# Moving every large operand buffer to the same address remainder as the weights

## The chip, the cores and the metric

The kernel runs on one core of a Trainium2 chip. The metric is the device time of one execution in microseconds (us). A core has a matrix engine (TensorE, PE in the profile, with its weight loads shown apart as PEld), a vector engine (VectorE, DVE), a scalar engine (ScalarE, ACT), GpSimd (POOL) and a queue engine that issues the transfers (SyncE, SP). On-chip memory (SBUF) has 128 partitions; a buffer takes the same range of bytes in each of them, and the addresses below are bytes within a partition.

## The reference

Four sequences of 576 tokens, eight heads of 64. The attention is masked by blocks of 64 tokens; its output, 2304 tokens of 512 features, goes through two feed-forward layers.

```
scores = where(block_i >= block_j, q k^T / 8, -1e9)      # per batch and head, 576 x 576
x = softmax(scores) v                                    # -> 2304 x 512
x = (sigmoid(x Wg) * (x Wv)) Wout                        # 512 -> 1536 -> 512
out = leaky_relu(x Win, 0.01) Wout2                      # 512 -> 2048 -> 512
```

## The kernel before

Every operand of a feed-forward product is kept as two parts, a high one and a low one, and a product of two tiles is three matmuls: high weights by high data, high weights by low data, low weights by high data (the loop over `wl, xl`, lines 1294 and 1142). The weights are the stationary operand (128 by 128), the data the moving one (up to 512 columns).

The 2304 tokens are three slices of 768, 512 and 1024 columns. The profile shows them as three stages. In stage 1 (about 50 to 364 us) and stage 2 (364 to 640 us) `half_unit` (line 1276) runs units of 12 matmuls, at 512 columns or, for the first 256 columns of the slice of 768, at 256. Units of kind gate, val and h read the layer's input; units of kind y and o read the intermediate `g`. Pieces of the attention of the later tokens stand between them. In stage 3 (from about 640 us) `pair_unit` (line 1109) multiplies the last 1024 columns as 2 by 2 blocks with seven products (`B11`, `T1`, `T2`, `B21`, `T3`, `B22`, `T4`) in place of eight; each product is two triples of matmuls at 512 columns. Its sums of blocks lie in buffers that stages 1 and 2 used before.

`Plan.order` (line 157) writes out one order of all instructions from fixed costs and due times, before the program is built. It knows no addresses.

Where a buffer lies: the program lays its pools out one behind the other in the order in which they are made, the constant tiles first, and rounds each start up to a multiple of 32 bytes. In the program before, the starts, and what is left of them after multiples of 256, are:

| remainder | buffers that TensorE reads |
|---|---|
| 32 | `w` (all weights, 63776 and on), `g`, `qk`, `v`, and in stage 3 `raw` (37152 and on) |
| 0 | `x1` (20736): input of stage 2; blocks `T1` and `B21` of stage 3 |
| 96 | `x0` (145760) and `xa` (162144): input of stage 1, `xa` also block `B22`; `sg` (170336): part of the intermediate of kind o, some blocks; `both` (182624): the attention's probabilities, blocks `B11`, `T2`, `T3`, `T4`; `acc` (215392): some blocks of stage 3 |
| 128 | `last` (16512) and `ident` (19072): two small operands of the attention |

All slices that the matmuls take from these buffers begin at a multiple of 256 bytes from the buffer's start. In the trace the names lose their numbers: `x` is `x0` and `x1`; below 364 us it is `x0`, later `x1`.

The names `mm`, `sc`, `tp` and `pa` are the banks that a matmul writes to, not what it computes: in stage 3 the feed-forward products of line 1147 write to `sc`, `tp` and `mm`.

Of the kernel before, what the change touches and what calls it, by code (L numbers as in the profile page):

```python
# [8 lines left out]
F32 = mybir.dt.float32  # L9
# [9 lines left out]
P = 128  # L19
# [205 lines left out]
def block_attention_then_two_mlps(  # L225
# [30 lines left out]
    def pool(name, bufs, **k):  # L256
        return ctx.enter_context(tc.tile_pool(name=name, bufs=bufs, **k))

    def ring(name, bufs, shape, dtype=F32, **k):
        return Ring(pool("p_" + name, bufs, **k), bufs, shape, dtype, name)  # L260

    out_hbm = out
    const = pool("const", 1)
# [19 lines left out]

    ident = const.tile([P, P], F32, name="ident")
    mask = const.tile([P, 4 * P + BLK], BF16, name="mask")
    x1 = const.tile([P, 4, 2, TN], F32R, name="x1")
    r_x = ring("x0", 4, [P, 2 * TN])
    r_xa = ring("xa", 2, [P, 4 * CUT])
    x0, xa, xt = [r_x.tile(F32R) for _ in range(4)], [r_xa.tile(F32R) for _ in range(2)], []
# [1159 lines left out]
    with tc.manual_schedule():  # L1449
        make_identity(nc, ident)  # L1450
        nc.gpsimd.memset(p_l[BLK:, (NKT - 1) * P:], 0.0)
        nc.gpsimd.memset(mask, 0.0)
        nc.gpsimd.memset(mask[:BLK, 4 * P:], MASK)
        warm = const.tile([P, 1], F32, name="warm")
        nc.vector.memset(warm, 0.0)
        nc.scalar.activation(warm, warm, AF.Exp)
        for o, e in plan.order():
            for t in o.uses:
                if t.ap is None:
                    t.ap = t.ring.pool.tile(t.ring.shape, t.dtype, name=t.ring.name)  # L1460
            if o.either:
                o.fn(e)
            else:
                o.fn()
# [39 lines left out]
```

## Time and profile before

| | us |
|---|---|
| median of 3 runs | 995.12 (994.21 to 996.48) |
| the profiled execution, as timed | 994.91 |
| its span in the trace | 993.1 |
| TensorE busy | 977.9 (98%) |
| VectorE busy | 779.5 (78%) |
| ScalarE busy | 550.3 (55%) |

The time as timed is 1.8 us above the span: what lies before the first and behind the last instruction. TensorE is busy in nearly the whole span and its granted clock is at full speed in all 40 slices of the page. A matmul's shown duration holds the time that it waits in the pipe behind its predecessor, so how fast matmuls follow each other is read from the difference of two starts, divided by the number of matmuls between them. The timeline below merges neighbours of one line and one name into one row, with the count behind.

### The profile page before, as it was taken

How to read it: one execution, taken by the hardware profiler on the slowest of the kernel's cores; microseconds unless marked ns; L12 is line 12 of the kernel's file. 1: busy time of each engine (PE TensorE's matmuls, PEld its weight loads, DVE VectorE, ACT ScalarE, POOL GpSimd, SP SyncE). 2: the span in 40 equal slices, each digit the busy share in tenths (PEclk: the TensorE clock that was granted, in tenths of full speed). 3: DMA queues.
4: the chain of work that ended last, by engine and by line, in shares of the span. 5: the costliest groups of instructions: out<-in, count | busy, mean ns of one | idle time of the engine just before them, and what ended most of it. 6: DMA issues, size and time to landing. Idle time of an engine off the chain costs nothing.

```text
span 993.1 us, 15675 instructions
## 1 busy us (share of the span) xinstructions
PE 977.9 (98%) x5468; PEld 779.7 (79%) x5468; DVE 779.5 (78%) x1658; ACT 550.3 (55%) x1103; POOL 166.1 (17%) x172
## 2 busy tenths in 40 slices
PE   7999999999999999999999999999999999999998
PEld 4688888878888878778777777788888877888886
DVE  6989989889989847777689888966437489958656
ACT  7988776676766526464566565443525144643521
POOL 2422001221102001232332223021002021100000
PEclk9999999999999999999999999999999999999999
DMA  8499786756876537979997877876565555665554
GB/s 207 135 292 270 264 289 219 258 186 242 265 258 197 208 116 268 299 273 298 281 296 266 303 265 243 280 267 220 173 200 186 187 170 160 204 204 182 193 185 154
DMA packets 92718, 227.52 MB, mean 229 GB/s; under 512 B 9952, under 2 KB 29920, under 8 KB 92640
## 3 DMA queue, kind: packets, MB, share of 16 engines
q1 hardware_dynamic: 92640, 226.53, 69.5%
q8 instruction: 43, 0.70, 0.3%
q14 instruction: 35, 0.29, 0.1%
HBM read 150.47 MB, written 76.02 MB: 228 GB/s over the span
## 4 chain that ended last, share of the span: by engine, by line
PE 94%; DVE 3%; DMA 1%; ACT 1%; SPq 0%; issue 0%; POOL 0%; DVEq 0%; ACTq 0%
PE mm L1299 48%; PE sc L1147 17%; PE tp L1147 9%; PE mm L1147 4%; PE tp L631 3%; PE sc L426 3%; PE pa L655 2%; PE tp L426 2%; PE tp L567 1%; DMA qk<-in_qk 1%; PE mm L655 1%; PE tp L582 1%; DMA w<-ds 1%; DVE x L1219 0%; SPq L330 0%; DVE g L353 0%
## 5 line engine op out<-in xcount | busy, mean ns | idle before, releaser
L1299 PE MATMUL mm<-x,w 128*128 128x512 f32 (+2 forms) x1008 | 236.9, 387 | 0.0
L1299 PEld LDWEIGHTS mm<-x,w 128*128 128x128 f32 x1008 | 179.8, 188 | 40.8 <-issue 5.2
L1299 PE MATMUL mm<-g,w 128*128 128x512 f32 (+1 forms) x792 | 164.0, 358 | 0.0
L1299 PEld LDWEIGHTS mm<-g,w 128*128 128x128 f32 x792 | 130.0, 189 | 23.4 <-issue 2.3
L1147 PE MATMUL sc<-both,w 128*128 128x512 f32 x480 | 130.6, 396 | 0.1
L1147 PEld LDWEIGHTS sc<-both,w 128*128 128x128 f32 x480 | 90.1, 188 | 21.8 <-ACT wf L340 0.5
L498 ACT ACTIVATE both<-both,nm 128x256 f32<-128x256 f32 (+5 forms) x148 | 84.1, 570 | 29.7 <-DVE nm L483 29.1
L899 POOL TENSOR_TENSOR wf<-mag,rnd 128x512 int32<-128x512 int32 x28 | 37.4, 1335 | 204.3 <-DVE w L353 149.5
L885 ACT ACTIVATE mag<-raw 128x512 f32<-128x512 f32 x68 | 45.5, 670 | 43.9 <-DVE wf L899 18.0
L1299 PE MATMUL mm<-xa,w 128*128 128x256 f32 x480 | 62.7, 281 | 0.0
L1299 PEld LDWEIGHTS mm<-xa,w 128*128 128x128 f32 x480 | 59.9, 188 | 3.3 <-issue 0.8
L353 DVE TENSOR_TENSOR g<-gf,g 128x512 fp32r<-128x512 f32 (+2 forms) x73 | 57.8, 793 | 3.5 <-ACT g L340 3.4
L518 POOL TENSOR_SCALAR both<-both,r 128x256 f32<-128x256 f32 (+6 forms) x54 | 34.9, 652 | 116.4 <-DVE r L511 97.0
L340 ACT ACTIVATE g<-gf 128x512 fp32r<-128x512 f32 (+2 forms) x61 | 40.0, 657 | 23.6 <-DVE gf L1330 11.9
L516 ACT ACTIVATE both<-both,r 128x384 f32<-128x384 f32 (+6 forms) x94 | 48.6, 566 | 6.9 <-DVE r L511 6.9
L483 DVE CUSTOM_DVE_ANT_0 both<-sc,mask 128x256 f32<-128x256 f32 (+6 forms) x101 | 39.4, 423 | 15.9 <-PE sc L426 15.8
L1360 DVE TENSOR_TENSOR acc<-mm,acc 128x512 f32<-128x512 f32 (+1 forms) x60 | 35.7, 598 | 18.1 <-PE mm L1299 17.7
L1219 DVE TENSOR_TENSOR x<-sc,x 128x512 f32<-128x512 f32 x44 | 30.2, 689 | 23.2 <-PE sc L1147 23.2
L426 PE MATMUL sc<-qk 64*128 64x384 f32 (+5 forms) x228 | 42.2, 415 | 5.9 <-DMA qk<-in_qk 5.9
L893 DVE SCALAR_TENSOR_TENSOR mag<-raw,mag 128x512 int32<-128x512 int32 x68 | 47.4, 698 | 0.3
L1299 PE MATMUL mm<-sg,w 128*128 128x512 f32 (+1 forms) x216 | 47.4, 355 | 0.0
L353 DVE TENSOR_TENSOR w<-wf,w 128x512 fp32r<-128x512 f32 x68 | 46.5, 684 | 0.2
(255 smaller groups left out, 1851.0 us busy)
## 6 DMA issues: line engine op xcount, KB each, us to landing
w<-wd SPq DMA_DIRECT2D x102, 512.0 KB, 4.6
raw<-in_w SPq DMA_DIRECT2D x68, 512.0 KB, 4.5
wd<-w SPq DMA_DIRECT2D x68, 512.0 KB, 4.2
ds<-raw SPq DMA_DIRECT2D x68, 512.0 KB, 5.2
w<-ds SPq DMA_DIRECT2D x68, 512.0 KB, 4.3
qk<-in_qk SPq DMA_DIRECT2D x32, 288.0 KB, 6.3
w<-wd SPq DMA_DIRECT2D x68, 128.0 KB, 3.8
v<-in_v SPq DMA_DIRECT2D x32, 160.0 KB, 3.5
```

The costliest lines, as they stand in the source:

```text
L340: nc.scalar.activation(dst(), src(), AF.Copy)
L353: engines[e].tensor_tensor(dst(), a(), f32(b()), ALU.subtract)
L426: nc.tensor.matmul(ps[row:row + nq, col:col + nk], lhsT=tqk[half, 0, q0:q0 + nq], rhs=tqk[half, 1, k0:k0 + nk], start=True, stop=True,)
L483: nc.vector.tensor_tensor_reduce(out=pt[:, n:n + width], in0=ps[:, col:col + width], in1=mask[:, 4 * P + BLK - width:] if masked else mask ...
L498: nc.scalar.activation(pt[:, :n], pt[:, :n], AF.Exp, bias=nm[:, k - 1:k], scale=-1.0, accum_out=sm[:, i:i + 1],)
L516: nc.scalar.activation(pt[:, :n], pt[:, :n], AF.Copy, scale=r[:, i:i + 1])
L885: op("act", c_act(n), lambda: nc.scalar.activation(mag[:], words(1).bitcast(F32), AF.Abs), [raw], [mag], [raw, mag], d - 8)
L893: op("dve", c_dve(n), lambda: nc.vector.scalar_tensor_tensor(out=mag[:].bitcast(I32), in0=words(1).bitcast(I32), scalar=-0x40000000, in1=m ...
L899: engines[e].tensor_tensor(wf[:].bitcast(I32), mag[:].bitcast(I32), rnd[:], ALU.add)
L1147: nc.tensor.matmul(p[:, :n], lhsT=wt[:, wl, at * P:(at + 1) * P], rhs=view[:, xl], start=first and k == 0 and wl + xl == 0, stop=k == 1 an ...
L1299: nc.tensor.matmul(ps[:, :n], lhsT=ws[:, wl, k * P:(k + 1) * P], rhs=srcs[k]()[:, xl, hs], start=k == 0 and wl + xl == 0, stop=k == 3 and ...
L1360: op("dve", c_dve(n), lambda: nc.vector.tensor_tensor(a(), ps[:, :n], a(), ALU.add), [ps], toks_a, [ps, *host], e)
```

## The change

A tile of 4 bytes, `warm`, is made before `x1` and no longer behind all other constants, and a pool with one tile of 48 floats (192 bytes), which nothing writes or reads, is made between `x1` and `x0`. Instructions, their order and their operands stay as they are; only addresses differ.

```
@@ constants and rings
     ident = const.tile([P, P], F32, name="ident")
     mask = const.tile([P, 4 * P + BLK], BF16, name="mask")
+    warm = const.tile([P, 1], F32, name="warm")
     x1 = const.tile([P, 4, 2, TN], F32R, name="x1")
+    pool("even", 1).tile([P, 48], F32, name="even")
     r_x = ring("x0", 4, [P, 2 * TN])
...
@@ before the planned order is issued
         nc.gpsimd.memset(mask[:BLK, 4 * P:], MASK)
-        warm = const.tile([P, 1], F32, name="warm")
         nc.vector.memset(warm, 0.0)
         nc.scalar.activation(warm, warm, AF.Exp)
```

## Rows read from the trace of the kernel before

**Rows 1.** The page, busy time: engine, us, share of the span, instructions.

```profile
PE   977.9 (98%) x5468; PEld 779.7 (79%) x5468; DVE 779.5 (78%) x1658; ACT 550.3 (55%) x1103; POOL 166.1 (17%) x172
```

**Rows 2.** The page, the chain that ended last, by engine.

```profile
PE 94%; DVE 3%; DMA 1%; ACT 1%; SPq 0%; issue 0%; POOL 0%; DVEq 0%; ACTq 0%
```

**Rows 3.** Timeline of TensorE in stage 3: start, us, line, operands, count.

```profile
645.98 11.07 PE L1299 MATMUL mm<-g,w 128*128 128x512 f32 x48
656.88 0.86 PE L1147 MATMUL tp<-x,w 128*128 128x512 f32 x3
...
700.29 0.86 PE L1147 MATMUL tp<-xa,w 128*128 128x512 f32 x3
...
712.18 0.40 PE L1147 MATMUL sc<-g,w 128*128 128x512 f32 x1
...
737.13 0.85 PE L1147 MATMUL sc<-both,w 128*128 128x512 f32 x3
...
741.93 0.62 PE L1147 MATMUL tp<-x,w 128*128 128x512 f32 x2
...
764.31 2.96 PE L1147 MATMUL sc<-both,w 128*128 128x512 f32 x12
...
769.91 0.40 PE L1147 MATMUL sc<-g,w 128*128 128x512 f32 x1
...
975.85 0.86 PE L1147 MATMUL mm<-raw,w 128*128 128x512 f32 x3
...
978.62 0.84 PE L1147 MATMUL mm<-raw,w 128*128 128x512 f32 x3
...
985.42 1.52 PE L1147 MATMUL sc<-g,w 128*128 128x512 f32 x6
```

**Rows 4.** Timeline of TensorE in stage 2, attention pieces between the units.

```profile
455.80 3.04 PE L1299 MATMUL mm<-x,w 128*128 128x512 f32 x12
458.67 0.93 PE L631 MATMUL tp<-ident,both 128*128 128x128 f32 x7
...
462.59 8.65 PE L1299 MATMUL mm<-x,w 128*128 128x512 f32 x36
471.17 0.70 PE L426 MATMUL sc<-qk 64*128 64x256 f32 x4
...
487.03 3.00 PE L1299 MATMUL mm<-g,w 128*128 128x512 f32 x12
489.87 0.93 PE L631 MATMUL tp<-ident,both 128*128 128x128 f32 x7
...
493.76 5.74 PE L1299 MATMUL mm<-g,w 128*128 128x512 f32 x24
499.34 0.86 PE L1299 MATMUL mm<-x,w 128*128 128x512 f32 x3
```

**Rows 5.** Timeline of TensorE in stage 1; a merged row can hold both widths.

```profile
103.57 1.58 PE L1299 MATMUL mm<-xa,w 128*128 128x256 f32 x12
...
107.73 1.58 PE L1299 MATMUL mm<-xa,w 128*128 128x256 f32 x12
...
124.37 16.88 PE L1299 MATMUL mm<-g,w 128*128 128x256 f32 x96
...
141.18 0.92 PE L426 MATMUL sc<-qk 64*128 64x384 f32 x4
```

**Rows 6.** Groups of TensorE by line and shape: count, busy us, mean ns.

```profile
L1299 PE MATMUL mm<-x,w 128*128 128x512 f32 x912 | 223.5, 397 | 0.0
...
L631 PE MATMUL tp<-ident,both 128*128 128x128 f32 x304 | 42.8, 274 | 0.8 <-ACT both L340 0.8
L1299 PE MATMUL mm<-sg,w 128*128 128x512 f32 x144 | 37.2, 393 | 0.0
```

**Rows 7.** Stretches: busy us (count) of each engine, granted clock, transfers.

```profile
656.90:990.00 333.10, 329.99 (x1417) 265.22 (x1415) 222.42 (x347) 135.69 (x225) 29.38 (x22) 1.00 0.59 192
...
820.00:840.00 20.00, 19.05 (x77) 13.65 (x76) 19.62 (x32) 8.72 (x15) 4.21 (x3) 1.00 0.56 179
```

More of the change, by code (lines that the diff above doesn't have):

```diff
@@ L285, in block_attention_then_two_mlps @@
     mask = const.tile([P, 4 * P + BLK], BF16, name="mask")
+    warm = const.tile([P, 1], F32, name="warm")
     x1 = const.tile([P, 4, 2, TN], F32R, name="x1")
+    pool("even", 1).tile([P, 48], F32, name="even")
     r_x = ring("x0", 4, [P, 2 * TN])
@@ L1453, in block_attention_then_two_mlps @@
         nc.gpsimd.memset(mask[:BLK, 4 * P:], MASK)
-        warm = const.tile([P, 1], F32, name="warm")
         nc.vector.memset(warm, 0.0)
```

## The prediction

> **What bounds the kernel now.** I read the page's busy times first: TensorE is busy 98% of the span, VectorE 78% [rows 1]. The chain that ended last says the same of the path: 94% of it is TensorE's own work [rows 2]. So the time is, to a few per cent, the sum of what its 5468 instructions take one behind the other, and a change that touches no instruction can only act through how closely matmuls follow each other. That is read from the timeline, as the difference of two starts over the count between them, and compared by the remainder of the moving buffer's address.
>
> Stage 3 gives all classes at 512 columns with the same weights [rows 3]:
> - Remainder 32, the weights' own: 48 matmuls on `g` from 645.98 to 656.88 take 10.90 us, 227.1 ns each. From 975.85 to 978.62 a run that mixes `raw`, `qk` and `g` needs 2.77 us for 12, 230.8 ns each; then, from 978.62 to 985.42, 6.80 us for 30, 226.7 ns. So such a run starts slow, for some nine to twelve matmuls, and settles.
> - Remainders 0 and 96 in turn, the usual case of this stage: 700.29 to 712.18, 51 matmuls in 11.89 us, 233.1 ns.
> - Remainder 96 alone: 21 in 4.80 us from 737.13 (228.6 ns), but 24 in 5.60 us from 764.31 (233.3 ns). It has two paces and does not leave the slow one in 24 matmuls.
>
> Remainder 0 alone stands in stage 2: 36 matmuls on `x1` from 462.59 to 471.17, 8.58 us, of which about 0.17 is the slow restart at both ends (how I get it is below): 233 to 234 ns [rows 4]. The buffers with the good remainder are of four kinds and the pace is one, so I take the address, not what the tile holds, for the cause.
>
> **What the change does to addresses.** `warm` (4 bytes, rounded to 32) now lies before `x1`: 20736 + 32 = 20768, which is 81 x 256 + 32. The constants keep their total, so `raw` to `v` with the weights stay at 32. The filler's 192 bytes bring `x0` from 145760 to 145952 = 570 x 256 + 32, and `xa`, `sg`, `both` and `acc` behind it go from 96 to 32 as well. The end moves from 227680 to 227872. `ident` and `last` stay at 128, so "every buffer" holds for the large ones only. No instruction is added, removed or moved; no wait, transfer or queue place changes.
>
> **Stage 3.** Between 656.9 and 990 TensorE is busy 329.99 us with 1417 instructions, 232.9 ns each [rows 7]. At 226.7 all 1428 products of this stage would save 1428 x 6.2 = 8.8 us. From that goes:
> - 1.9 us for the 21 places of this stage (counted in the timeline) where a product waited or restarted and its first matmul is followed late, at 0.09 us each, the restart of stage 2 (below); that excess is in the mean and stays;
> - 0.5 us for settling again at about a dozen separate ones, 9 matmuls by 4 to 5 ns each, from the run at 975.85;
> - 0.6 us in the one part where VectorE is the bound: from 820 to 840 it is busy 19.62 of 20.00 us and TensorE only 19.05 [rows 7], and the stretch before looks alike. What some 30 us of products gain there, 2%, comes back as waiting.
>
> Left: 5.8 us. The bounds are 8.8 - 1.9 = 6.9 (settled at once, nothing given back) and 4.4 (VectorE gives back 2% of 100 us and not of 30).
>
> **Stage 2.** Here units of 12 are cut apart by transposes of the attention. Behind such a cut, 12 on `x1` take 455.80 to 458.67, 2.87 us, and 12 on `g` take 487.03 to 489.87, 2.84 us [rows 4]: the unit ends about when the good pace is reached, and 0.03 is all. 2.87 against 12 x 233 = 2.80 gives the restart of 0.07 to 0.09. Later units of one run gain more: the second of the 24 on `g` from 493.76 to 499.34 takes 5.58 - 2.84 = 2.74, where a later one of the 36 on `x1` takes (8.58 - 2.87 - 0.09) / 2 = 2.81: 0.07. Of the 912 matmuls on `x` at 512 columns [rows 6] 480 are on `x1` (the 40 units gate, val and h by 12). About 29 units begin a run and 11 do not (counted in the timeline): 29 x 0.03 + 11 x 0.07 = 1.6 us. The bounds: 0.9 (0.03 each, rounded down, for all) and 3.1 (480 x 6.4 ns, settled at once).
>
> **Stage 1.** The units alternate 12 matmuls at 256 columns and 12 at 512. On `xa` and `x0`, remainder 96, one takes 107.73 - 103.57 = 4.16 us. On `g`, remainder 32, four take 141.18 - 124.37 = 16.81, less 0.09 for the cut behind the last, 4.18 each [rows 5]. So the change costs 0.02 on each of 40 units: 0.8 us lost; between 0 and 1.6 from what the starts, printed to 0.01, allow over 40 units. What the 512 columns gain once they settle, the 256 columns give away.
>
> **The rest.** 144 matmuls on `sg` at 512 columns [rows 6] go from 96 to 32: 0.3 us gained, between 0 (they stay unsettled) and 0.9 (6.6 ns each). Transposes with `both` as the weights (304 of them in the largest group [rows 6], 408 in all) and the products of probabilities and `v`, some 380 instructions, also see `both` move. No row shows them at another remainder; the nearest are the classes of the wide products, whose ends are 6.4 ns apart over 512 columns and which in stage 1 cancel. I take 0, and plus or minus 2 us (3 ns by the sum of both, some 790) as ends. VectorE's and ScalarE's operands in these buffers move too; TensorE covers them nearly everywhere, I take 0.
>
> **Sum.** 5.8 + 1.6 + 0.3 - 0.8 = 6.9 us. Against the profiled execution's own 994.91 us (span 993.1 and 1.8 around it) that is 988.0; the median of the runs shown is 0.2 us above that execution, so I say 988.2.
>
> **Rivals.**
> 1. *Nothing changes, 995.1.* For it: the paces may belong to the mixture of buffers, the order of reads or the settled state before, not to the address; 96 alone shows both 228.6 and 233.3 [rows 3], so the remainder isn't the whole story. Against it: no run at 32 longer than a dozen stays slow, and no run on `x1` gets fast. 8%. The page "SBUF — State Buffer" of the Trainium skill, in "Who interferes with whom", says that TensorE's two read ports are its own and independent and that "PE and ACT never wait on anyone"; by that rule no address could slow a matmul and this rival would hold. The three paces in this trace, 226.7, 228.6 and 233 ns for one shape, speak against it.
> 2. *The gain is given back as waiting, 991.2.* If VectorE holds TensorE not in 30 but in 100 us of stage 3, and stage 2 gains nothing because its units are released by transfers and VectorE, what is left is 4.4 + 0.3 - 0.8 = 3.9 us: 995.1 - 3.9 = 991.2. For it: VectorE is at 19.62 of 20 us in one place and at 222 of 333 over the stage [rows 7], so other places can be like it. Against it: the chain has only 3% VectorE and 1% transfers [rows 2]. 12%.
> 3. *Slower, 999.* One mechanism: the settled pace is lost when blocks of different hosts follow each other, because equal remainders make weights and data meet more often than before. Then all 32s run at their first dozen's pace: in stage 3 the matmuls that now run at 226.7 or 228.6 go to 231 to 233, some 2 us lost; stage 1 loses the 1.6 of its bound and stage 2 about 0.4 on its `g` units: 995.1 + 4 = 999. It decides from the point where no run gets past its first twelve. For it: the first 12 from 975.85 at 230.8 ns. Against it: that very run goes on over three kinds of buffer and settles. 5%.
>
> **How the numbers follow.** The forecast has 75%, the rivals 8, 12 and 5. Its own range, from the bounds of the terms, is 985 to 991: stage 3 up to 1.1 more, stage 2 1.5 more, `sg` 0.6 on the good side not all at once, 2 us either way for the attention, against 1.4 and 0.7 less in stages 3 and 2 on the bad side. Rival 2 lies at its edge, so 985.0 to 991.6 holds eight cases in ten. A difference under 0.2% (2.0 us, the spread of the runs shown is 2.3) can't be told from none. Faster by more than that: the forecast and nearly all of rival 2, 0.86; the same: 0.09; slower: 0.05.
>
> **What would show it.** In stage 3, runs over changing buffers at 226.7 ns, so that triples stand 0.68 us apart and not 0.70, and the run that now begins at 975.85 begins about 6 us earlier; TensorE's busy sum from 656.9 on down by 6 us; stage 2 shorter by 1.6 to 2; units of stage 1 at 4.18 and not 4.16. The prediction is wrong if triples on `both` or `x1` still stand 0.70 apart, if rows with a wait on VectorE grow by more than 2 us in stage 3, or if transposes have another distance than now.

## The result and the profile after

The changed kernel takes 987.93 us (median of 4 runs, 986.15 to 988.29) against 995.65 before (4 runs, 994.21 to 996.48): a ratio of 0.992 with a 95% interval of 0.9903 to 0.9938. The forecast was 988.2. The profiled execution took 986.15 us, its span is 984.4.

First the page, busy time and the chain; they answer to [rows 1, 2].

```profile
PE 969.9 (99%) x5468; PEld 780.4 (79%) x5468; DVE 778.8 (79%) x1658; ACT 549.6 (56%) x1103; POOL 164.8 (17%) x172
...
PE 94%; DVE 2%; DMA 2%; ACT 1%; issue 0%; SPq 0%; ACTq 0%
```

The counts of instructions are those of before; TensorE's busy sum fell by 8.0 us, about what the span fell by (8.7), and the other engines' sums moved by 1.3 us or less.

The timeline of TensorE in stage 3, the places of [rows 3]: the run of 48 on `g`, the turns between `xa`, `both` and `x1`, and the long run near the end. Columns as there.

```profile
643.07 11.04 PE L1301 MATMUL mm<-g,w 128*128 128x512 f32 x48
653.95 0.84 PE L1149 MATMUL tp<-x,w 128*128 128x512 f32 x3
...
696.11 0.84 PE L1149 MATMUL tp<-xa,w 128*128 128x512 f32 x3
696.78 1.52 PE L1149 MATMUL sc<-both,w 128*128 128x512 f32 x6
698.14 0.84 PE L1149 MATMUL tp<-x,w 128*128 128x512 f32 x3
698.83 0.84 PE L1149 MATMUL sc<-both,w 128*128 128x512 f32 x3
...
967.14 0.84 PE L1149 MATMUL mm<-raw,w 128*128 128x512 f32 x3
...
976.66 1.52 PE L1149 MATMUL sc<-g,w 128*128 128x512 f32 x6
```

From 696.11 to 698.83 there are 12 matmuls over three buffers in 2.72 us, 226.7 ns each; before, the same turns went at 233.1. The run from 967.14 has no slow start any more; its predecessors on `sg` now have the same remainder: 42 matmuls in 9.52 us, 226.7 ns. The run on `g`, at 32 before and after, takes 10.88 against 10.90, which says little: a repeat of the changed kernel has 10.90 there.

The same stretch of the program and the part where VectorE is busiest, as in [rows 7] (each moved with the program):

```profile
654.00:981.60 327.60, 324.05 (x1417) 264.67 (x1415) 222.34 (x347) 135.28 (x225) 29.28 (x22) 1.00 0.60 196
815.00:835.00 20.00, 18.94 (x79) 14.14 (x78) 19.64 (x32) 9.54 (x16) 4.17 (x3) 1.00 0.55 178
```

1417 instructions now take 324.05 us and not 329.99: 5.9 us. VectorE still fills its 20 us. TensorE's idle time in the stretch grew from 3.11 to 3.55 us. The listed waits of TensorE from 638 us on, first before, then after (what it waited for, us in total, times, longest):

```profile
PE tp L1147 <- DMA w<-ds: 1.1, 1, 1.1
PE sc L1147 <- DVE x L1219: 0.8, 1, 0.8
PE tp L1147 <- DVE g L353: 0.8, 1, 0.8
PE tp L1147 <- DVE x L353: 0.8, 1, 0.8
...
PE tp L1149 <- DMA w<-ds: 1.8, 3, 1.1
PE tp L1149 <- DVE x L355: 0.9, 1, 0.9
PE sc L1149 <- DVE x L1221: 0.8, 1, 0.8
```

Waits on VectorE fell from 2.4 to 1.7 us; those on transfers of weights grew from 1.1 to 1.8.

Stage 2, to be laid beside [rows 4]:

```profile
455.29 3.00 PE L1301 MATMUL mm<-x,w 128*128 128x512 f32 x12
458.13 0.93 PE L633 MATMUL tp<-ident,both 128*128 128x128 f32 x7
...
462.01 8.44 PE L1301 MATMUL mm<-x,w 128*128 128x512 f32 x36
470.38 0.70 PE L428 MATMUL sc<-qk 64*128 64x256 f32 x4
```

12 on `x1` behind a cut take 2.84 us (2.87 before), 36 take 8.37 (8.58).

Stage 1, to be laid beside [rows 5]:

```profile
103.31 1.60 PE L1301 MATMUL mm<-xa,w 128*128 128x256 f32 x12
104.75 2.91 PE L1301 MATMUL mm<-x,w 128*128 128x512 f32 x12
107.49 1.60 PE L1301 MATMUL mm<-xa,w 128*128 128x256 f32 x12
```

A unit takes 4.18 us, 0.02 more than before: 1.44 for the 256 columns, 2.74 for the 512.

Since both programs issue the same matmuls in the same order, each distance from one start to the next can be subtracted from its counterpart. Summed (worked out from the two traces, by row over the distances that stay under 243 ns at 512 columns and 137 ns at 256 in both, so without waits and restarts; these and the pieces of the attention, which the last row holds too, differ between any two executions by some tenths):

| stage, matmuls | count | before, ns | after, ns | us |
|---|---|---|---|---|
| 1, 256 columns, 96 to 32 | 511 | 117.2 | 119.5 | +1.2 |
| 1, 512 columns, 96 to 32 | 460 | 229.6 | 228.5 | -0.5 |
| 2, 512 columns, 0 to 32 (`x1`) | 421 | 233.1 | 227.9 | -2.2 |
| 2, 512 columns, others | 332 | 229.9 | 228.5 | -0.45 |
| 3, 0 to 32 | 244 | 232.6 | 226.8 | -1.4 |
| 3, 96 to 32 | 732 | 231.6 | 226.9 | -3.4 |
| 3, 32 and unmoved | 483 | 230.1 | 227.0 | -1.5 |
| all of stage 1 / 2 / 3 | | | | +0.2 / -3.0 / -6.0 |

### The profile page after: what moved, and what is told of

The parts are those of the page before. It is cut to its first block, busy times and chain, and to the rows that moved or that the text cites. A ratio compares the mean times of both kernels' runs of the same rounds, so it can differ in the third digit from the quotient of the medians.

```text
span 984.4 us, 15675 instructions
## 1 busy us (share of the span) xinstructions
PE 969.9 (99%) x5468; PEld 780.4 (79%) x5468; DVE 778.8 (79%) x1658; ACT 549.6 (56%) x1103; POOL 164.8 (17%) x172
## 4 chain that ended last, share of the span: by engine, by line
PE 94%; DVE 2%; DMA 2%; ACT 1%; issue 0%; SPq 0%; ACTq 0%
PE mm L1301 47%; PE sc L1149 18%; PE tp L1149 9%; PE mm L1149 4%; PE sc L428 3%; PE tp L633 3%; PE pa L657 2%; PE tp L428 2%; DMA w<-ds 1%; PE tp L569 1%; PE mm L657 1%; PE tp L584 1%; PE pa L428 1%; DVE x L1221 0%; DMA qk<-in_qk 0%; ACT both L518 0%
## 5 line engine op out<-in xcount | busy, mean ns | idle before, releaser
L1301 PE MATMUL mm<-x,w 128*128 128x512 f32 (+2 forms) x1008 | 234.3, 384 | 0.0
L1149 PE MATMUL sc<-both,w 128*128 128x512 f32 x480 | 128.2, 390 | 0.1
```

Of the source, the lines that this page charges most:

```text
L1149: nc.tensor.matmul(p[:, :n], lhsT=wt[:, wl, at * P:(at + 1) * P], rhs=view[:, xl], start=first and k == 0 and wl + xl == 0, stop=k == 1 an ...
L1301: nc.tensor.matmul(ps[:, :n], lhsT=ws[:, wl, k * P:(k + 1) * P], rhs=srcs[k]()[:, xl, hs], start=k == 0 and wl + xl == 0, stop=k == 3 and ...
```

## The experiments

Three theories of why. A: the distance between the address of the data and that of the weights, modulo 256, sets the pace, and distance 0 is the fast one. B: the data's own remainder, 32, sets it. C: it is enough that neighbours have one remainder among themselves. The kernels below are the changed one with the edit shown; the kernel before, measured beside them, had medians of 994.9, 994.9 and 995.0. Distance always means data minus weights.

**One half: `x1` alone.**

```diff
-    pool("even", 1).tile([P, 48], F32, name="even")
```

> Half of the change: warm stands before x1, no filler. x1 is at remainder 32, x0, xa, sg, both and acc stay at 96. Theory A (what counts is the remainder of the data against that of the weights, and a run of equal ones settles at 226.7 ns) and theory B (what counts is the data's own remainder, 32) expect the same here: stage 2 shorter by about 2.2 us (421 matmuls on x1 at 228 and not 233 ns), stage 3 by at most 1 us, since its runs still change between 32 and 96; 992.0 to 993.0 against 995.6 before. Theory C (no address counts alone, only that neighbours have the same remainder) expects the same stage 2 unchanged, since x1's runs there are among themselves already at 233 ns: 995.

Measured: 992.52 us, ratio 0.9974 (0.9963 to 0.9984). Stage 2's matmuls on `x1` went from 233.1 to 228.6 ns (1.9 us); stage 3 stayed where it was, to 0.01 us. Its timeline, `x1` now at 32 between `both` and `xa` at 96:

```profile
700.27 0.86 PE L1148 MATMUL tp<-x,w 128*128 128x512 f32 x3
700.97 0.86 PE L1148 MATMUL sc<-both,w 128*128 128x512 f32 x3
701.67 0.86 PE L1148 MATMUL tp<-x,w 128*128 128x512 f32 x3
702.36 0.86 PE L1148 MATMUL mm<-x,w 128*128 128x512 f32 x3
```

Triples 0.70 apart: a good buffer among bad ones gains nothing. C expected nothing in stage 2 and is wrong: `x1`'s runs were of one remainder before too, and slow.

**The other half: the filler alone.**

```diff
-    warm = const.tile([P, 1], F32, name="warm")
     x1 = const.tile([P, 4, 2, TN], F32R, name="x1")
+    warm = const.tile([P, 1], F32, name="warm")
```

> The other half: the filler alone. x0, xa, sg, both and acc go to 32, x1 stays at 0. A and B: stage 1 as with the whole change (within 0.3 us of before), stage 2 as before but for 0.5 us on sg and g, stage 3 shorter, but less than by the whole change (6.0 us), as the 240 matmuls on x1 at 233 ns stay and break the settled runs on both: 2 to 3.5 us; 992 to 993.5. If the two halves add up to the whole change, their gains sum to 7.7; if settling over changing buffers is what stage 3 gains by, the sum falls short by 2 us or more.

Measured: 990.94 us, ratio 0.9964 (0.9951 to 0.9976), a little better than expected. Stage 3 gained 4.0 us, more than the 2 to 3.5 expected. (The profiled execution is the slowest of the five, 992.83: attention pieces of stages 1 and 2 took 1.5 us longer in it, so only sums over the same matmuls are compared.) The timeline shows why not 6:

```profile
702.09 1.52 PE L1149 MATMUL sc<-both,w 128*128 128x512 f32 x6
703.45 0.86 PE L1149 MATMUL tp<-x,w 128*128 128x512 f32 x3
704.15 0.85 PE L1149 MATMUL sc<-both,w 128*128 128x512 f32 x3
704.84 0.86 PE L1149 MATMUL tp<-x,w 128*128 128x512 f32 x3
705.54 0.86 PE L1149 MATMUL mm<-x,w 128*128 128x512 f32 x3
...
706.94 2.89 PE L1149 MATMUL sc<-both,w 128*128 128x512 f32 x12
709.67 0.86 PE L1149 MATMUL mm<-x,w 128*128 128x512 f32 x3
```

Six on `both` take 1.36 us (226.7 ns) until a triple on `x1`, still at 0, comes: 0.70 for it and 0.69 for the next on `both`. In stage 3 the halves give 0.0 and 4.0 and the whole 6.0: the last 2 us exist only when no buffer in the run is off. By the medians the halves gain 2.4 and 4.0, 1.3 less together than the whole's 7.7, where 2 or more had been put down.

**All large buffers at 96, the weights too.**

```diff
+    const.tile([P, 16], F32, name="shift")
     warm = const.tile([P, 1], F32, name="warm")
     x1 = const.tile([P, 4, 2, TN], F32R, name="x1")
```

> The change, and a further 64 bytes ahead of x1: all large buffers, weights and data, are at remainder 96. Theory A (relative): as the change, 987.5 to 988.5, runs at 226.7 ns. Theory B (the data's own remainder): the paces that data at 96 had before, 228.6 or 233.3 ns, 991 (1428 x 2 ns more in stage 3) to 998. Theory C (equality of neighbours): as A here.

Measured: 986.9 us, ratio 0.9918 (0.9904 to 0.9932). The run on `g`:

```profile
642.72 11.04 PE L1302 MATMUL mm<-g,w 128*128 128x512 f32 x48
653.60 0.84 PE L1150 MATMUL tp<-x,w 128*128 128x512 f32 x3
654.28 0.84 PE L1150 MATMUL sc<-both,w 128*128 128x512 f32 x3
```

48 in 10.88 us, 226.7 ns, with data at 96. The time is 0.6 us below the range that A gave. B is wrong: 96 is as good as 32 if the weights are there too.

**The weights alone at 96.**

```diff
+    pool("ahead", 1).tile([P, 16], F32, name="ahead")
     r_w = ring("w", 7, [P, 2, 4 * P], F32R)
+    pool("behind", 1).tile([P, 48], F32, name="behind")
```

> The change, but the weight tiles w alone are at remainder 96 (64 bytes ahead of them, 192 behind); all data stay at 32, so they stand 64 below the weights. Theory A (relative): the settled 226.7 ns is gone; at the paces of other remainders (228.6 to 233.3) 991 to 998. Theory B (the data's own remainder) and theory C (equal neighbours): 987.5 to 988.5.

Measured: 999.74 us, ratio 1.0049 (1.0036 to 1.0061): slower than before, and a little above what A allowed. First the run on `g`, then stage 1:

```profile
649.20 11.36 PE L1303 MATMUL mm<-g,w 128*128 128x512 f32 x48
660.40 0.86 PE L1151 MATMUL tp<-x,w 128*128 128x512 f32 x3
...
104.28 1.53 PE L1303 MATMUL mm<-xa,w 128*128 128x256 f32 x12
105.65 2.96 PE L1303 MATMUL mm<-x,w 128*128 128x512 f32 x12
108.44 1.53 PE L1303 MATMUL mm<-xa,w 128*128 128x256 f32 x12
```

All data still lie at 32 and share one remainder, and 48 matmuls take 11.20 us, 233.3 ns, from first to last. Only A stands. But at 256 columns this distance (192) is the better one: 12 in 1.37 us, 114 ns, against 119.5 at distance 0.

**The other distances.** The same edit with other sizes: 56 floats ahead and 8 behind (weights at 0), 24 and 40 (128), 32 and 32 (160), 40 and 24 (192).

> The change with the weights at remainder 0: data at 32 are 32 above them. Each distance of data and weights has its own pace, and the whole kernel runs at one of them, so one run reads it at 512 and at 256 columns. Theory A1 (only distance 0 modulo 256 is the fast one at 512 columns): 229 to 234 ns, 990 to 1000 us. Theory A2 (the distance counts modulo 128): this is the unknown distance 32, also 229 to 234.

> The change with the weights at remainder 128: data are 160 above them modulo 256. A1: 229 to 234 ns at 512 columns, 990 to 1000 us. A2 (modulo 128): the same paces as with the weights at 0, at both widths. At 256 columns distance 192 gave 114 ns, 64 gave 117 and 0 gave 119.5; 160 should lie near 192, 114 to 117, if the pace changes smoothly with the distance.

> The change with the weights at remainder 160: data are 128 above them. A1: 229 to 234 ns, 990 to 1000 us. A2 (the distance counts modulo 128): 226.7 ns and 119.5 ns as with the change, 987 to 988.5 us.

> The change with the weights at remainder 192: data are 96 above them. A1: 229 to 234 ns, 990 to 1000 us, and at 256 columns something from 114 to 118. A2 (modulo 128): the pace of x1 before, whose distance was 224: 233 ns, 997 to 1000 us.

The run of 48 on `g` in the kernels with the weights at 0, at 192 and at 128 (the slowest), and then in the one with them at 160, where half of 256 lies between data and weights:

```profile
649.06 11.36 PE L1303 MATMUL mm<-g,w 128*128 128x512 f32 x48
660.26 0.86 PE L1151 MATMUL tp<-x,w 128*128 128x512 f32 x3
...
652.48 11.36 PE L1303 MATMUL mm<-g,w 128*128 128x512 f32 x48
663.68 0.63 PE L1151 MATMUL tp<-x,w 128*128 128x512 f32 x2
...
651.55 11.41 PE L1303 MATMUL mm<-g,w 128*128 128x512 f32 x48
662.79 0.86 PE L1151 MATMUL tp<-x,w 128*128 128x512 f32 x3
```

```profile
649.25 11.36 PE L1303 MATMUL mm<-g,w 128*128 128x512 f32 x48
660.45 0.86 PE L1151 MATMUL tp<-x,w 128*128 128x512 f32 x3
...
103.56 1.58 PE L1303 MATMUL mm<-xa,w 128*128 128x256 f32 x12
104.98 2.96 PE L1303 MATMUL mm<-x,w 128*128 128x512 f32 x12
```

| data minus weights, modulo 256 | 512 columns, run of 48, ns | 256 columns, stage 1 mean, ns | us |
|---|---|---|---|
| 0 (the change) | 226.7 | 119.5 | 987.93 |
| 0 (all at 96) | 226.7 | 119.5 | 986.9 |
| 32 | 233.3 | 116.8 | 999.76 |
| 96 | 233.3 | 119.7 | 1003.43 |
| 128 | 233.3 | 118.7 | 1000.49 |
| 160 | 234.2 | 117.6 | 1004.72 |
| 192 | 233.3 | 114.1 | 999.74 |

Distance 0 is alone at 512 columns; 224 (`x1` before) had 233 and 64 (`both` before) two paces. Distance 0 was run with two pairs of remainders (32 and 32, 96 and 96), with the same paces; the other distances of the table with data at 32 alone, so that the distance and not the pair sets their paces is not shown. A2, a period of 128, falls by distance 128, which is at 233.3 and not at 226.7. At 256 columns the paces go up and down with no order that I see; 160 isn't near 192, and 96 has 119.7 and not 114 to 118, against what I had put down, and distance 0 is one of the two worst. Three of the four times lie above the 1000 us that A1 allowed. By the start to start sums against the kernel before, stage 1 lost at both widths with the weights at 192 (1.3 us at 256 columns, 2.8 at 512) and at 160 (0.6 and 2.1); with them at 128, the slowest, it lost 2.9 at 512 columns alone, and stages 2 and 3 another 1.8 and 4.4. I had not added these up.

**A version for both widths.** Stage 1's first 256 columns want distance 192, stage 3's blocks in the same tiles want 0. Longer tiles allow both:

```diff
-    r_xa = ring("xa", 2, [P, 4 * CUT])
+    r_xa = ring("xa", 2, [P, 4 * CUT + 64])
...
-        a, c = (x[:].rearrange("p (k l n) -> p k l n", l=2, n=n) for x, n in ((xa[k // 2], CUT), (x0[k], TN)))
+        a, c = (
+            x.rearrange("p (k l n) -> p k l n", l=2, n=n) for x, n in ((xa[k // 2][:, 48:48 + 4 * CUT], CUT), (x0[k][:], TN))
+        )
```

> The change as it is, beside the next kernel on the same chip: 987 to 988.5 us.

> The change, with the tiles xa 256 bytes longer each, and stage 1's first 256 columns kept 192 bytes into them (remainder 224, distance 192 from the weights), while stage 3 uses the same tiles from their start (remainder 32). Theory A (each distance and width has its own pace: 226.7 ns at 512 columns for 0, 114.2 ns at 256 columns for 192, against 119.5 for 0): stage 1 shorter by up to 480 x 5.3 ns = 2.5 us, by 1.5 if the 512 columns behind lose some of their settling; the rest as with the change; 1.5 to 2.5 us below the change, about 985.5. Rival (the 114.2 ns needed all units, y's too, at distance 192): 256 columns on xa stay at 117 or more, under 1.2 us below the change.

Measured side by side: the change again 986.76 us (986.53 to 986.93), ratio 0.9913 (0.9898 to 0.9928), just below its expected range; this version 985.36 (984.44 to 985.88), ratio 0.9899 (0.9882 to 0.9915). The two intervals overlap; the runs, four of each on the same chip, don't. The gain is 1.4 us, under the 1.5 to 2.5 I expected. Stage 1 of it:

```profile
104.04 1.58 PE L1303 MATMUL mm<-xa,w 128*128 128x256 f32 x12
105.46 2.88 PE L1303 MATMUL mm<-x,w 128*128 128x512 f32 x12
108.18 0.99 PE L1303 MATMUL mm<-xa,w 128*128 128x256 f32 x7
```

A unit takes 4.14 us against 4.18, as 12 at 256 columns now take 1.42 (117.0 ns over the stage) and 12 at 512 behind them 2.72, 226.7 ns. The start to start sums give 1.1 us at 256 and 0.45 at 512 columns. So the rival was right on the pace: the 114 ns of distance 192 didn't come (the gain is above its 1.2 us by what the 512 columns gave). Two things differ from the kernel with 114 ns: these units stand between units at distance 0, and the remainders are 224 and 32 in place of 32 and 96. No run tells which of them it is. It is the fastest of the versions run.

## Why the prediction was right

- **The mechanism.** That the remainder of data against weights sets the pace was read from three classes of one trace; the runs show that equal remainders are the fast case at 512 columns, with six of the eight distances (in steps of 32), each on a whole kernel, and rule out the two readings (B and C) that the prediction couldn't tell from it, since its weights all lay at 32. The prediction spoke of equal remainders, which is A, but its rows alone would have fitted B as well.
- **The number.** 988.2 against 987.93 is closer than the terms were. By the two profiled executions the stages gained 8.8 us in all, where the forecast had 6.9; by the medians the gain is 7.7, as the profiled execution is the fastest of its four. That the median came out within 0.3 us is partly luck.
- **Stage 3, 5.8 us forecast, 6.0 measured.** The triples stand 0.68 apart, over changing buffers. Matmuls that follow closely gained 6.3 us, for 8.8 - 1.9 - 0.5 = 6.4 forecast: the restarts stayed (a restarted product is followed after some 335 to 340 ns in both traces). 0.4 us came back (the forecast had 0.6), but not where the forecast had it: the listed waits on VectorE fell by 0.7 us, and at 963 to 965 us, where TensorE now waited for weights, the products stand 0.5 us further apart. In the version for both widths only 0.1 came back, so the forecast's reason for this term was wrong and its size is chance.
- **Stage 2, 1.6 for `x1`, 2.2 measured; the sign was 1.6 to 2 for the stage, 3.0 measured.** Mis-sized was the gain of each unit. The 23 units behind a cut gained 0.044 us on average (the one shown 0.03, as forecast), the 12 behind other units on `x1` 0.08 and not 0.07, and the 5 behind units on `g` or `sg`, which now inherit a settled run, 0.07 and not 0.03. The rest of the stage, `sg` and the neighbours on `g`, gained 0.45, of which the forecast had only a part of its 0.3 for `sg`. Another 0.4 us of the stage lies in the attention's pieces and the edges; nothing shows that it is the address and not the spread of two executions.
- **Stage 1, 0.8 lost, 0.2 measured in all.** The units do take the 0.02 more; +1.2 and -0.5 make 0.7, with `sg` in both (0.3 lost at 256 columns, 0.3 gained at 512). The rest, 0.5, came back at the start and in attention pieces; `x1_only`, which moves nothing that stage 1's units read, differs there by 0.45 the other way, so this is spread.
- **The attention, 0 forecast.** Start to start, the transposes of line 631 (250 distances inside their groups) have 115.5 ns before and after, and the products of probabilities and `v` at 384 columns (68) 134.3, although `both` went from 96 to 32. So the 0 was right, and the address counts here in the wide products only.
- **The rivals.** No change fell: nothing changed but addresses, and the same instructions ran between 226.7 and 234.2 ns. The Trainium skill states in "SBUF — State Buffer", "Who interferes with whom", that TensorE's two read ports are independent and that TensorE never waits on anyone. The prediction read this as a rule by which no address could slow a matmul, and so read it doesn't hold here; whether the two ports are what meets, no run shows. The gain wasn't given back as waiting. The mechanism of the slower rival, equal remainders meeting more often, has the wrong sign; 999 did appear, where remainders were unequal everywhere.
- **Slips.** The lower bound of stage 2, 0.03 for all 40 units, is 1.2 and not 0.9; by the trace 28 units begin a run and 12 don't. I wrote that the run of 975.85 would begin 6 us earlier; that is stage 3's own share, and with stage 2's it began 8.7 earlier, at 967.14. The loops over `wl, xl` stand at lines 1146 and 1298 of the kernel before, `pair_unit` at 1123 and `order` at 149, not at the lines given ahead.

## What to carry to other kernels

When one engine fills the span and a change moves only addresses, compare start to start distances of one shape by the address of what it reads, before looking anywhere else: the price of the other layouts stood here in the trace of before. Here, with a 128-column weight load under a 512-column matmul, data and weights with the same remainder modulo 256 bytes were worth 3% per matmul (226.7 against 233 ns), only if all buffers of a run had it; at 256 columns the same layout was among the worst, so the widths have to be weighed by their counts.

## What the runs showed of the hardware that was not expected

- Distance 0 modulo 256 of moving and stationary operand is the only one of eight (in steps of 32) that gave 226.7 ns at 512 columns; the seven others lie at 229 to 234 ns. A run at distance 0 can need some nine to twelve matmuls to settle behind other work or behind matmuls at another distance (230.8, then 226.7 ns [rows 3]), but not always: in the kernel with the filler alone 12 on `both`, three matmuls behind one on `x1`, took 2.73 us, 227.5 ns each.
- The order is another one at 256 columns: 114 ns at distance 192, 119.5 at 0. The attention's narrower products showed no effect (134.3 ns at 384 columns with 64 columns of weights, at distance 64 before and 0 after).
- At distance 64 the same run can go at 228.6 or at 233.3 ns for over 20 matmuls [rows 3]; what decides between them was not found, nor what in the chip makes the distance count. That it is the reading of weights beside the stream of data is a guess; no run took the weight loads away.
